# Loads of a backward recurrence: moved from SyncE's queue to ScalarE's, with an earlier compaction and a tile of its own for extra sums

## The chip, the cores and the metric

The kernel runs on one core of a Trainium2 chip. The metric is device time in microseconds (us) of one execution; lower is better. TensorE (PE) does matmuls and transposes, VectorE (DVE) and ScalarE (ACT) work element by element, GpSimd (POOL) does copies and issues DMAs, and SyncE (SP) only issues DMAs. "SPq", "ACTq" and so on in profile lines are the engines' sequencers.

## The reference

The inputs are x (2048 tokens of 640), a memory of 8 rows, the weights Wq, Wk, Wv, Wo (32 heads of 128) and the three weights of a gated feed-forward network. All are bfloat16. The forward function is

```
xn  = layernorm(x)
mem = mem0
for i in range(64):                      # segments of 32 tokens
    h = concat(mem, xn[32 i : 32 i + 32])          # 8 + 32 rows
    q, k, v = h Wq, h Wk, h Wv                     # 32 heads of 128
    p = softmax(mask(q k^T * 128**-0.5))           # memory rows see all, token rows are causal
    o = (p v) Wo
    mem, out[i] = o[:8], o[8:]
s = concat(out)
g = silu(FFN(xn))
y = x + s * g
```

The kernel returns y and the gradients of all nine inputs for a given gradient of y. The memory makes the forward pass a chain of 64 steps, and the backward pass a second chain of 64 steps in the other direction: the gradient of a segment's memory rows is needed before the segment ahead of it can be worked on.

## The kernel before

The kernel goes through stages, which the profile shows one after the other (times from the start of the span): layer norm and the network forward (0 to 370 us), the forward recurrence (370 to 1690), a prologue of the backward pass (to 1826), the backward sweep (`phase4_Abwd`, 1826 to 3240), the gradients of Wq, Wk, Wv and of the token rows (`phase6_Awgrads`, to 4330), that of Wo (to 4650), and the network's backward pass (to 4945).

**One step of the sweep**, `chain(t, gap)`, t from 63 down to 0, takes the gradient of the memory rows of its segment, already turned (`hx`, in profile rows the copy at L1335), and on TensorE does in this order:

- `packed_half` twice and `packed_sel`: the 8 rows times Wo, for all heads. VectorE and ScalarE copy the halves to `sg` (rows `gs` in the profile).
- `vgrad` (L1199): the value gradients of all 40 rows of the segment. Its first part multiplies the probabilities of the 32 token rows, `prx`, with their gradient rows `xr`; its second part multiplies those of the memory rows, `prm`, with `sg`. These value gradients "ride" in the step because the 8 memory rows of them go on along the chain.
- `dprob_m` (its bank at L1278): the gradient of the memory rows' probabilities, after VectorE has made `gmT` from `sg` (L1264). ScalarE copies the result to `dPT` (L1282).
- transposes of `dPT`, and VectorE's softmax gradient `gpr` ... `dS`; the key gradients `gkv`; a transpose of `dS` that ScalarE copies to `dST` (profile rows `dSTm`, L1306); the query gradients from `dST`.
- between these, the `packed_out` groups: value, key and query gradients times the turned weights, summed in one bank. `fold_add` (ScalarE copies one half, VectorE adds, L339 and L341) makes the sum `fs` (tile `fsum`), `fold_turn` (L357) turns it into the next step's input, and `fold_store` has POOL store it (to `GWO` and `GXV`, L348).

`load_g(t - 1)` fetches what the next step's vgrad needs: `xr` from `GOS` or `GX`, `prf` (the same tokens' probabilities, 256 KB, from `PR`) and four small `prm` loads from `PM`. `xr` and `prf` lie in one large tile, and the profile names both `gor`. `prx_copy(t - 1)` compacts `prf` to `prx` with two copies on POOL (L1192, L1193).

**The gaps.** The token rows' own work needs no chain, and is put into the steps' gaps by hand: 157 *units* (a tile of 120 rows and four heads each) pass through `ld` (loads on SP, ahead of time, into a ring of tiles), `turn` (transposes on TensorE, three ScalarE copies to `gvT` and `gOT`, a store by POOL to `VTD`), `dprob` (`gdp`, L1391), `dsoft` (VectorE, a store by POOL to `DSR`) and `gmem` (ScalarE copy `gks`, a store by POOL to `GXP`). `gap_of` says which unit does what in which gap:

```
G1: turn 2nd unit, gmem_ld last unit of t + 1, dprob 1st unit
G2: dprob 2nd, turn 3rd, dsoft 1st        G3: dsoft 2nd, gmem_ld 1st, extra every 4th step
G4: dprob 3rd, turn 1st of the next step  G5: gmem_ld 2nd     G6: dsoft 3rd
```

`extra(m, bank)` in every fourth step multiplies the value gradients of four steps' memory rows, collected in `lv`, with the turned Wv, adds the halves into a tile `fsum` and has POOL store it to `GXV`. The tag `fsum` has one buffer, which `gpr`, `gu`, the step's sum and the extra sum share.

**The order.** `in_order` fixes each engine's instructions in the sweep to the written order, so a statement's place in `chain` is its place in its engine's queue. DMAs are issued by the engine that they are written for: `nc.sync` is SP, `nc.scalar` is ScalarE, `nc.gpsimd` is POOL.

**The weight gradients.** `Fetch` loads 8 x 22 units, each with the softmax gradient `dS` (from `DSR`), the probabilities `Pr` and rows `g`, `q`, `k` into a ring of `NB` places of the tile `land`. TensorE transposes `dS` (L1648), multiplies the three kinds (`r6p`, L1658), ScalarE and VectorE copy the results, and later groups multiply them with the layer's input (L1715, L1736).

Of the kernel before, what the change touches and what calls it, by code (L numbers as in the profile page):

```python
# [9 lines left out]
BF16 = mybir.dt.bfloat16  # L10
# [313 lines left out]
def packed_out(k, pm, x, W, first, last, i0=0, i1=16):  # L324

    nq = x.shape[2]
    for i in range(i0, i1):
        for a in range(2):
            for b in range(2):
                h = 16 * a + i  # L330
                p0 = 32 * (2 * a + b)
                k.nc.tensor.matmul(pm[p0:p0 + nq, 0:320], x[:, h, :], W[:, h, 320 * b:320 * b + 320],  # L332
                                   start=(first and i == 0), stop=(last and i == 15),
                                   tile_position=(0, p0), skip_group_check=True)


def fold_add(k, pm, up, fs):

    k.nc.scalar.copy(up, pm[64:128, 0:320])  # L339
    for c in (0, 160):  # L340
        k.nc.vector.tensor_tensor(fs[:, c:c + 160], pm[0:64, c:c + 160], up[:, c:c + 160], ALU.add)  # L341
    return fs
# [746 lines left out]
def phase4_Abwd(k, out2, W0, W4, WT, own, ps, banks):  # L1089
    nc, tc = k.nc, k.tc  # L1090
    D, DC, S, H, HD, T = k.D, k.DC, k.S, k.H, k.HD, k.T
# [5 lines left out]
    for s in range(3):  # L1097
        t0 = (2, 0, 1)[s]
        n = (T - 1 - t0 + 2) // 3
# [10 lines left out]
    with tc.tile_pool(name="gst", bufs=1) as st, tc.tile_pool(name="gchain", bufs=1) as ch, \  # L1110
# [67 lines left out]
                nc.gpsimd.dma_start(rows[64 * a:64 * a + 8].rearrange("r (g c) -> r g c", g=2),  # L1178
                                    k.GOS[t // 4, 2 * a:2 * a + 2, 0:8, t % 4, :].rearrange("g r c -> r g c"))

        def load_g(t):
            tl, s = t // 3, t % 3
            nc.sync.dma_start(xr, k.g_rows(t))
            nc.sync.dma_start(prf, k.PR[tl][32 * s:32 * s + 32].rearrange("q (g h) c -> g q (h c)", g=4))
            for g in range(4):
                nc.sync.dma_start(prm[32 * g:32 * g + 8],
                                  k.PM[t, g // 2].rearrange("(q b h) c -> b q h c", q=8, b=2)[g % 2])

        def prx_copy(t):
# [11 lines left out]

        def extra(m, bank):
            packed_out(k, bank, lv, WvT, True, True)
            fs = fold_add(k, bank, up, ch.tile([64, 320], BF16, name="fsum", tag="fsum"))
            for b in range(2):
                nc.gpsimd.dma_start(k.GXV[128 * m:128 * m + 128, 320 * b:320 * b + 320].rearrange("(t r) d -> t r d", r=32)[:, 24:32],
                                    fs[32 * b:32 * b + 32, :])
# [26 lines left out]
        def chain(t, gap):  # L1234
# [30 lines left out]
                                      pg[:, :, 2 * a:2 * a + 2, :].rearrange("p j g q -> p q g j"))  # L1265
            vgrad(vb, sg, prm, 8, 4, 8, False)
            nc.sync.dma_start(k.GOS[t // 4, :, :, t % 4].rearrange("g r c -> (g r) c"), sg)
            if t > 0:
                load_g(t - 1)
            for g, e in ((0, 's'), (2, 'v'), (1, 's'), (3, 'v')):  # L1270
                k.copy(gv[:, 8 * g:8 * g + 8, :], vb[g], eng=e)
            nc.gpsimd.tensor_copy(lv[:, :, 8 * (t % 4):8 * (t % 4) + 8], gv[:, :, 32:40])
# [7 lines left out]
            dprob_m(1)  # L1280
            dPT = ch.tile([40, 2, P], BF16, name="dPT", tag="seq")
            nc.scalar.copy(dPT[:], psd.rearrange("p a q h -> p a (q h)"))  # L1282
            gap("G1")
            packed_out(k, pm, gv32, WvT, True, False, 0, 5)
            ps2 = bview(bC, P, 2, 40, bf=True)
# [36 lines left out]
            with nc.allow_non_contiguous_dma(reason="mem rows of dS"):  # L1322
                for a in range(2):
                    for (c0, c1, d0) in ((0, 8, nx + 8 * s), (8, 40, 32 * s)):
                        (nc.sync, nc.gpsimd)[a].dma_start(k.DSR[tl][nx + 8 * s:nx + 8 * s + 8, 16 * a:16 * a + 16, d0:d0 + c1 - c0],
                                                          dS[:, a, c0:c1])
            packed_out(k, pm, gkT, WkT, False, False, 4, 16)
            gap("G3")
            packed_out(k, pm, gqT, WqT, False, True)
# [5 lines left out]
                nc.vector.tensor_copy(goxs[(t - 1) % 2][:, :, 0:8], pt[:])  # L1335
            fold_store(nc.gpsimd, k.m_rows(k.GWO, t - 1) if t > 0 else out2f, fs)
            fold_store(nc.gpsimd, k.GXV[32 * t:32 * t + 24, :], fs, 8)
            if t > 0:
                prx_copy(t - 1)
            gap("G6")  # L1340

        uu = {}
# [102 lines left out]
        def gap_of(t):  # L1445
            def at(f, tt, i0, i1=None):
                b = batch.get(tt, ())
                for u in b[i0:i0 + 1 if i1 is None else i1]:
                    f(*u)

            def gap(g):
                if g == "W0":
                    ride_ld(t - 1)
                elif g == "G1":
                    at(turn, t, 1)
                    at(gmem_ld, t + 1, 2)
                    at(dprob, t, 0)
                elif g == "G2":
                    at(dprob, t, 1)
                    at(turn, t, 2)  # L1460
                    at(dsoft, t, 0)
                elif g == "G3":
                    if t > 0:
                        load_xp(t - 1)
                    at(dsoft, t, 1)
                    at(gmem_ld, t, 0)
                    if t % 4 == 0:
                        extra(t // 4, ps.tile([P, 512], F32, name="exb", tag="x", bufs=5))
                elif g == "G4":
                    at(dprob, t, 2)  # L1470
                    at(turn, t - 1, 0)
                elif g == "G5":
                    at(gmem_ld, t, 1)
                elif g == "G6":
                    at(dsoft, t, 2)
                if t == 0 and g == "G1":
                    fetch.append(Fetch(k, W0))
                if t == 0 and g in ("G1", "G2"):
                    fetch[0].to(2 if g == "G1" else 3)
                if t == 0 and g == "G3":  # L1480
                    fetch[0].w(0)
                for i in range(WARM.get(g, 0)):
                    nc.tensor.matmul((bA if g in ("W1", "G2") else bB)[:], k.ident[:], WqT[:, 0, 0:512], start=True, stop=True)
            return gap
# [41 lines left out]
        for i in range(len(pro) + 2):  # L1526
            for f, o in ((turn, 0), (dprob, 1), (dsoft, 1), (gmem, 2)):
                if 0 <= i - o < len(pro):
                    f(*pro[i - o])
                if f is not dsoft and not (f is dprob and i % 3):  # L1530
                    next(work, None)
            if 0 <= i - 2 and (i - 2 + 6 < len(pro) or i >= len(pro) - 2):
                ld_next()
            if 1 <= i < 17:
                h0 = 2 * (i - 1)
                nc.sync.dma_start(WvT[:, h0:h0 + 2, :], k.WVT[:, h0:h0 + 2, :])
            if i == 8:
                chain_consts()
                ride_ld(T - 1)
            if i == 16:  # L1540
                ride(T - 1)
            if i == len(pro):
                for _ in work:
                    pass
                loads(T - 1)
                load_q(T - 1)
                load_xp(T - 1)
                load_g(T - 1)
                prx_copy(T - 1)
        load_k(T - 1)  # L1550
        for t in range(T - 1, -1, -1):
# [8 lines left out]
class Fetch:  # L1560

    def __init__(self, k, W0):
        self.k, self.NB = k, 5
        NF = k.NTL - 2
        self.units = [(qd, tl) for qd in range(8) for tl in [NF, NF + 1] + list(range(NF - 1, -1, -1))]
        self.st, self.Ws, self.n = {}, {}, 0
        t = W0.tile([P, 5 * self.NB * 512 + 8 * k.D], BF16, name="land", tag="w0")
        four = lambda ap: ap.rearrange("p (h c) -> p h c", h=4)
        b = [[t[0:120, 512 * (5 * i + j):512 * (5 * i + j) + 512] for i in range(self.NB)] for j in range(5)]
        self.dS, self.P = [[four(x) for x in y] for y in b[0:2]]  # L1570
        self.rows = dict(zip("gqk", b[2:5]))
        c = 5 * self.NB * 512
        self.ws = [four(t[:, c + 4 * k.D * i:c + 4 * k.D * (i + 1)]) for i in range(2)]
# [10 lines left out]
    def ld(self, u):  # L1584
        k, nc = self.k, self.k.nc
        qd, tl = self.units[u]
        c0, h0 = qd * 512, qd * 4
        n = k.geo(tl)[3]
        dS, Pr = self.dS[u % self.NB], self.P[u % self.NB]
        nc.sync.dma_start(dS[0:n], k.DSR[tl][:, h0:h0 + 4, :])  # L1590
        nc.sync.dma_start(Pr[0:n], k.PR[tl][:, h0:h0 + 4, :])
        rw = []
        for nm in ("g", "q", "k"):
            r = self.rows[nm][u % self.NB]
            src = k.g_src(tl, c0, c0 + 512) if nm == "g" else k.x_src(tl, nm, c0, c0 + 512)
            k.load_x(r, 0, src, nc.sync)
            if nm == "q":
                t0, (ns, nm_, nx, n) = 3 * tl, k.geo(tl)
                nc.sync.dma_start(r[nx:n], k.QVM[t0:t0 + ns, :, qd // 2, 0, 512 * (qd % 2):512 * (qd % 2) + 512].rearrange("t r c -> (t r) c"))
            else:  # L1600
                k.load_m(r, tl, nm, c0, c0 + 512, nc.gpsimd)
            rw.append(r)
        self.st["l", u] = (dS, Pr, rw)
# [7 lines left out]
def phase6_Awgrads(k, X, W0, fetch, out0, out3, out4, out5):  # L1611
# [6 lines left out]
    NF = NTL - 2  # L1618
    NS = k.NR - 120 * NF
    R = 384  # L1620
    NB = 5
    assert NS == 8 * NF and NW == NF and (96 * NF) % R == 0 and S - 96 * NF == P
    st, Ws, cnt = fetch.st, fetch.Ws, dict(w=0, s=0, g=0, x=0)
    units, ld_to, ld_w = fetch.units, fetch.to, fetch.w
    with tc.tile_pool(name="h6i", bufs=3) as io, tc.tile_pool(name="h6", bufs=1) as hp, \
# [140 lines left out]
            s1(u0 + 2)  # L1766
            yield

        ld_to(5)
        for p in range(3):  # L1770
            gv_ld(p)
        for _ in head(0):
# [589 lines left out]
```

## Time and profile before

| | |
|---|---|
| median of 3 runs | 4944.16 us (4942.93 to 4951.85) |
| the profiled execution | 4946.79 us, of which the span 4944.8 us |
| mean granted TensorE clock | 0.945 |
| busy share of the span | PE 90%, PEld 57%, DVE 46%, ACT 32%, POOL 42% |
| instructions | 165433 |
| DMA | 853.19 MB, mean 173 GB/s |
| backward sweep, 1826 to 3240 us | PE busy 1169.17 of 1414 us, granted clock 0.86 |
| weight gradients, 3240 to 4330 us | PE busy 1015.63 of 1090 us, granted clock 0.98 |

The views of the profile are read like this. A row of waits says which engine stood still at which line, `<-` what released it, then the sum in us, how often, and the longest; "bank <- POOL prx" is a wait of a matmul into `bank` for POOL's writing of `prx`, and "DMA gor<-PR" is the landing of a transfer from `PR` into `gor`. A row of a timeline has start and duration in us, engine, line, operation, written from read tile, shape, and in square brackets the idle time before it with its releaser. The granted clock is the share of full speed that the throttle left to TensorE. Durations of DMA_DIRECT2D rows on an engine's queue are those of issuing, not of the transfer.

### The profile page before, as it was taken

The numbers are of one execution on the slowest core, as the hardware profiler recorded it, in microseconds if no ns is written. First come the engines' busy times: TensorE is split into PE (matmuls) and PEld (weight loads), VectorE is DVE, ScalarE is ACT, GpSimd is POOL, SyncE is SP. The second block draws the span as 40 slices with busy tenths as digits, with TensorE's granted clock in tenths as the row PEclk, the third lists the DMA queues.
The fourth block names the chain that finished last, engine by engine and source line by source line (L and its number), as shares of the span: only waits on it lengthen the run. The fifth ranks groups of instructions, "written<-read, shape, count | busy, mean of one in ns | idle before, by whom it ended". The sixth has DMA issues, their size and how long they took to land.

```text
span 4944.8 us, 165433 instructions
## 1 busy us (share of the span) xinstructions
PE 4464.1 (90%) x66872; PEld 2806.8 (57%) x66872; DVE 2257.3 (46%) x7188; ACT 1576.9 (32%) x4328; POOL 2075.0 (42%) x3512
## 2 busy tenths in 40 slices
PE   8998999999998878887778888879999999999999
PEld 4545555555555545555555555555555666667675
DVE  8635666666665344443434444343333333411461
ACT  5433555555444323222222222222222222200000
POOL 6533555555555134444434444353333333311440
PEclk9999999999999988888888888889999999999999
DMA  8774666666555776666655655585444555559783
GB/s 273 220 248 123 177 179 181 179 180 182 168 169 167 166 208 178 186 182 176 176 165 168 170 167 168 146 201 139 132 133 130 145 151 151 179 169 230 161 188 95
DMA packets 1004226, 853.19 MB, mean 173 GB/s; under 512 B 527910, under 2 KB 870490, under 8 KB 1001500
## 3 DMA queue, kind: packets, MB, share of 16 engines
q1 hardware_dynamic: 798227, 572.69, 42.0%
q0 software_dynamic: 122960, 221.40, 15.0%
q10 hardware_dynamic: 82275, 48.52, 3.8%
q8 instruction: 528, 8.65, 0.8%
q14 instruction: 236, 1.93, 0.1%
HBM read 496.51 MB, written 304.56 MB: 162 GB/s over the span
## 4 chain that ended last, share of the span: by engine, by line
PE 40%; DMA 12%; issue 5%; POOL 4%; DVE 3%; SPq 1%; ACT 1%; ACTq 0%; POOLq 0%; DVEq 0%
PE wg L1736 10%; PE bank L332 6%; PE g L1715 4%; DMA land<-DSR 4%; PE oa L1884 4%; PE wa L2272 2%; PE bank L313 2%; PE r6p L1658 1%; PE pgxb L2205 1%; DMA GXV<-fsum 1%; PE bank L1278 1%; PE t6g L1691 1%; DMA kT<-QVS 1%; DMA kT<-GOS 1%; PE t L1648 1%
## 5 line engine op out<-in xcount | busy, mean ns | idle before, releaser
L1736 PE MATMUL wg<-gr,hr 128*128 128x512 bf16 x2400 | 521.7, 379 | 0.3 <-DMA hr<-HRO 0.3
L313 PEld LDWEIGHTS <-hx 128*32 128x32 bf16 x10240 | 256.0, 99 | 251.6 <-issue 49.6
L1736 PEld LDWEIGHTS <-hr 128*128 128x128 bf16 x2400 | 233.9, 98 | 279.3 <-DMA hr<-HRO 0.6
L1715 PE MATMUL g<-land,ghacc 128*128 128x320 bf16 x2048 | 326.7, 305 | 0.0
L1378 POOL DMA_DIRECT2D VTD<-gvT x176 | 126.5, 719 | 420.4 <-ACT gvT L1377 396.3
L90 DVE CAST wgo<-wg 128x512 bf16<-128x512 f32 x72 | 49.8, 692 | 471.7 <-PE wg L1736 471.7
L90 DVE CAST stg<-bank 128x512 bf16<-128x512 f32 x256 | 177.1, 692 | 157.4 <-PE bank L313 154.2
L886 POOL DMA_DIRECT2D OR<-xv x163 | 89.8, 551 | 364.2 <-ACT xv L92 341.6
L332 PE MATMUL bank<-WvT,gv 128*32 128x320 bf16 x4096 | 233.6, 390 | 0.0
L1715 PEld LDWEIGHTS <-ghacc 128*128 128x128 bf16 x2048 | 193.1, 99 | 65.8
L1673 POOL DMA_DIRECT2D GSP<-grs x48 | 25.5, 542 | 466.0 <-ACT grs L1665 466.0
L818 ACT ACTIVATE xP<-xsp,xnm 120x120 bf16<-120x120 f32 (+1 forms) x540 | 186.6, 374 | 26.4 <-DVE xnm L800 23.6
L313 PE MATMUL bank<-WoT,hx 128*32 128x512 bf16 x2560 | 183.0, 441 | 11.8 <-DVE hx L1335 11.1
L838 POOL TENSOR_TENSOR xP<-xP,xrz 120x480 bf16<-120x480 bf16 x163 | 161.1, 989 | 64.9 <-DVE xrz L837 40.3
L92 ACT CAST wgo<-wg 128x512 bf16<-128x512 f32 x48 | 28.1, 586 | 465.4 <-PE wg L1736 394.4
L246 POOL DMA_DIRECT2D land<-KS x256 | 144.9, 571 | 65.9 <-PE r6p L1658 51.0
L332 PE MATMUL bank<-Wo,oTm 128*32 128x320 bf16 x4032 | 154.5, 307 | 18.9 <-DVE oTm L689 18.8
L92 ACT COPY ghacc<-t6g 128x384 bf16<-128x384 bf16 (+1 forms) x176 | 82.6, 469 | 275.5 <-PE t6g L1691 272.7
L332 PE MATMUL bank<-WkT,kT 128*8 128x320 bf16 x4096 | 161.5, 299 | 2.8 <-DVE kT L1245 1.7
L313 PE MATMUL bank<-Wq,hx 128*32 128x512 bf16 x2560 | 161.6, 381 | 0.0
L313 PE MATMUL bank<-Wv,hx 128*32 128x512 bf16 x2560 | 161.6, 381 | 0.0
L332 PEld LDWEIGHTS <-gv 128*32 128x32 bf16 x4096 | 120.8, 120 | 63.7
(392 smaller groups left out, 10832.0 us busy)
## 6 DMA issues: line engine op xcount, KB each, us to landing
QVS<-stg SPq DMA_DIRECT2D x128, 256.0 KB
kT<-VTD SPq DMA_DIRECT2D x64, 320.0 KB
PR<-xP POOLq DMA_DIRECT2D x168, 120.0 KB
VTD<-gvT POOLq DMA_DIRECT2D x168, 120.0 KB
land<-DSR SPq DMA_DIRECT2D x168, 120.0 KB
land<-PR SPq DMA_DIRECT2D x168, 120.0 KB
OR<-xv POOLq DMA_DIRECT2D x163, 120.0 KB
orr<-OR SPq DMA_DIRECT2D x14, 1280.0 KB
```

Of the source, the lines that this page charges most:

```text
L90: return nc.vector.tensor_copy(out, in_)
L92: return nc.scalar.copy(out, in_)
L246: eng.dma_start(d, src if src.shape[0] > 1 else src[0])
L313: k.nc.tensor.matmul(bank[32 * g:32 * g + 32, :], x[:, dc, :], W[:, dc, c0:c0 + 512], start=(dc == 0), stop=(dc == k.DC - 1), tile_positio ...
L332: k.nc.tensor.matmul(pm[p0:p0 + nq, 0:320], x[:, h, :], W[:, h, 320 * b:320 * b + 320], start=(first and i == 0), stop=(last and i == 15), ...
L818: nc.scalar.activation(Pb[0:n, j, 0:n], sp[0:n, j, :], ACT.Exp, bias=nmx[0:n, j:j + 1], scale=k.scale, accum_out=Z[0:n, j:j + 1])
L838: eng.tensor_tensor(Pb[0:n, :, 0:n], Pb[0:n, :, 0:n], bc_last(rz[0:n], n), ALU.mult)
L1378: nc.gpsimd.dma_start(k.VTD[tl][:, :, h0:h0 + 4, :], vTq[:])
L1715: nc.tensor.matmul(pg[:], ring[:, i, j, r0:r0 + P], Ws[qd][i][:, j, 320 * h:320 * h + 320], start=(i == 0 and j == 0), stop=(i == 1 and j ...
L1736: nc.tensor.matmul(pw[:], hr[:, tl, dc * P:(dc + 1) * P], grs[i][:, tl, :], start=(tl == 0), stop=(tl == NF - 1))
L1884: nc.tensor.matmul(ac[j][i][:], orr[:, w, jj * P:(jj + 1) * P], gow[:, w, 320 * i:320 * i + 320], start=(w == 0), stop=(w == NW - 1))
L2272: nc.tensor.matmul(accs[i][:], xn_all[:, tt, dc * P:(dc + 1) * P], gtok[:, tt, 432 * f:432 * f + 432], start=(tt == 0), stop=(tt == NT - 1))
```

## The change

- `load_g(t - 1)` gets the queue as an argument. In the steps ScalarE issues it, right behind its copy to `dPT`; before, SP issued it behind the store to `GOS`. `prf` is now loaded ahead of `xr`. The first load, ahead of the sweep, stays on SP.
- `prx_copy(t - 1)` moves from the end of the step to its middle, behind the stores of the memory rows of `dS` and ahead of the second part of the key gradients' `packed_out`.
- `extra` writes its sums to the first 64 partitions of `lv`, no longer to a tile of tag `fsum`.
- `dprob` of a step's first unit moves from gap G1 to gap W1, behind vgrad and ahead of `dprob_m`.
- `Fetch` has six places for five, so one more unit is loaded ahead. Of a unit's loads, `Pr` and the `g` rows are issued by ScalarE; SP keeps four.

```diff
-        def load_g(t):
+        def load_g(t, q):
             tl, s = t // 3, t % 3
-            nc.sync.dma_start(xr, k.g_rows(t))
-            nc.sync.dma_start(prf, k.PR[tl][32 * s:32 * s + 32].rearrange("q (g h) c -> g q (h c)", g=4))
+            q.dma_start(prf, k.PR[tl][32 * s:32 * s + 32].rearrange("q (g h) c -> g q (h c)", g=4))
+            q.dma_start(xr, k.g_rows(t))
             for g in range(4):
-                nc.sync.dma_start(prm[32 * g:32 * g + 8],
+                q.dma_start(prm[32 * g:32 * g + 8],
                                   k.PM[t, g // 2].rearrange("(q b h) c -> b q h c", q=8, b=2)[g % 2])
...
         def extra(m, bank):
             packed_out(k, bank, lv, WvT, True, True)
-            fs = fold_add(k, bank, up, ch.tile([64, 320], BF16, name="fsum", tag="fsum"))
+            fs = fold_add(k, bank, up, lv[0:64].rearrange("p h c -> p (h c)")[:, 0:320])
...
             nc.sync.dma_start(k.GOS[t // 4, :, :, t % 4].rearrange("g r c -> (g r) c"), sg)
-            if t > 0:
-                load_g(t - 1)
...
             nc.scalar.copy(dPT[:], psd.rearrange("p a q h -> p a (q h)"))
+            if t > 0:
+                load_g(t - 1, nc.scalar)
             gap("G1")
...
                         (nc.sync, nc.gpsimd)[a].dma_start(k.DSR[tl][nx + 8 * s:nx + 8 * s + 8, 16 * a:16 * a + 16, d0:d0 + c1 - c0],
                                                           dS[:, a, c0:c1])
+            if t > 0:
+                prx_copy(t - 1)
             packed_out(k, pm, gkT, WkT, False, False, 4, 16)
...
             fold_store(nc.gpsimd, k.GXV[32 * t:32 * t + 24, :], fs, 8)
-            if t > 0:
-                prx_copy(t - 1)
             gap("G6")
...
+                elif g == "W1":
+                    at(dprob, t, 0)
                 elif g == "G1":
                     at(turn, t, 1)
                     at(gmem_ld, t + 1, 2)
-                    at(dprob, t, 0)
...
-                load_g(T - 1)
+                load_g(T - 1, nc.sync)
...
-        self.k, self.NB = k, 5
+        self.k, self.NB = k, 6
...
-        nc.sync.dma_start(Pr[0:n], k.PR[tl][:, h0:h0 + 4, :])
+        nc.scalar.dma_start(Pr[0:n], k.PR[tl][:, h0:h0 + 4, :])
...
-            k.load_x(r, 0, src, nc.sync)
+            k.load_x(r, 0, src, nc.scalar if nm == "g" else nc.sync)
...
-    NB = 5
+    NB = fetch.NB
...
-        ld_to(5)
+        ld_to(NB)
```

## The prediction

> **What bounds the kernel now.** I read the table by stage first, then TensorE's waits, then the queues behind the longest of them. In the table by stage the columns after the window are its length and the busy time (count) of PE, PEld, DVE, ACT and POOL, then the granted clock, the DMA share and GB/s. The backward sweep and the weight gradients are the two stages that the diff touches:
>
> ```profile
> 1826.00:3240.00 1414.00, 1169.17 (x28160) 778.34 (x28160) 574.84 (x2863) 391.63 (x1150) 599.47 (x1143) 0.86 0.60 169
> 3240.00:4330.00 1090.00, 1015.63 (x8742) 648.91 (x8738) 407.00 (x893) 293.26 (x577) 422.34 (x753) 0.98 0.55 152
> ```
>
> TensorE sets both ends: 83% busy in the sweep, 93% after it. What a change can bring at an equal clock is its idle time, 245 us and 74 us. The sweep is 64 steps of 22.0 us. TensorE's waits name the idle time (total, times, longest):
>
> ```profile
> PE bank L1199 <- POOL prx L1193: 98.9, 40, 11.8
> PE t L1648 <- DMA land<-DSR: 55.9, 51, 4.2
> PE bank L357 <- DVE fsum L341: 44.0, 36, 4.3
> PE gvpt L1374 <- DMA kT<-QVS: 29.7, 16, 3.3
> PE bank L1278 <- DVE gmT L1264: 20.2, 55, 0.5
> PE gvpt L1374 <- DMA kT<-QVX: 12.0, 9, 2.6
> ```
>
> The first is the compaction of the probabilities. The timeline of POOL, then of PE, at the seam of two steps:
>
> ```profile
> 2103.97 1.04 POOL L348 DMA_DIRECT2D GWO<-fsum  x2
> 2104.99 1.02 POOL L348 DMA_DIRECT2D GXV<-fsum  x2
> 2106.01 0.41 POOL L1192 COPY prx<-gor 128x256 bf16<-128x256 bf16 x1
> 2106.35 0.24 POOL L1193 COPY prx<-gor 128x64 bf16<-128x64 bf16 x1
> ```
>
> ```profile
> 2106.64 0.17 PE L1199 MATMUL bank<-prx,gor 32*128 32x40 bf16 x1 [1.60 <-POOL prx L1193]
> ```
>
> The copies stand behind four store issues of 2.06 us that need the step's last sum; their input landed long before. TensorE idles 1.60 us for them. The unit loads (kT rows) are late because of SP's queue, which the waits of SP in the sweep show:
>
> ```profile
> SPq L1365 <- DMA gor<-PR: 100.4, 38, 3.9
> SPq L1174 <- DMA gor<-PR: 62.4, 25, 4.6
> SPq L272 <- DMA gor<-GOS: 58.5, 25, 3.1
> SPq L1174 <- DMA gor<-GOS: 37.3, 16, 3.5
> ```
>
> Lines L1365, L272 and L1174 load other tiles, yet wait for the landing of load_g's (the gor rows). In the built program all DMAs of SP and ScalarE take eight completion semaphores in turn, and an issue waits until the last DMA of its semaphore has landed. With the two gor<-GX rows (21.3 and 10.2) this is 290 us, 4.5 us per step.
>
> **The change part by part.**
>
> *Compaction in mid step.* It removes 98.9 us of waits. The copies (0.65 us) now wait for the landing of prf. On SP's ring it came 9.35 us (median) after the issue, worked out from issue and semaphore times; issued at the end of the dPT copy, that is some 12 us ahead of the next seam. POOL's stores queued behind them (DSR, GXP, VTD, then GWO and GXV) are late by up to 4 us, and the last two still follow the last sum. Next late at the seam is ScalarE's copy of sg (vgrad's second half); in steps without the wait, vgrad's first matmul came 0.04 us after that copy began. I take −95; bounds −107 (8 us of waits named otherwise at the same line) and −80.
>
> *Place for the extra sums.* One step in four writes two sums in one tile, and the second waits for the store of the first: 53.9 us of VectorE's waits in the sweep, 13 times. TensorE's L357 wait in these steps is 34.9 of the 44.0 (summed by step). Gone: −35, bounds −38 and −28. lv is next written about 10 us later, when its stores have landed.
>
> *dprob into W1.* Its eight matmuls stand where TensorE waited for gmT: 20.2 us in 55 steps. Part of the steps carry no first unit: −14, bounds −20 and +5 (dPT comes later by dprob where the wait was short).
>
> *load_g off SP.* SP loses, per step, 0.59 + 0.57 + 4 × 0.36 = 2.6 us of issue and waits of 4.5 us. Late unit loads cost TensorE 29.7 + 12.0 and, for GOS rows and the line's rest, 8: 49.7. I take −34; bounds −49.7 and −10, as ScalarE's DMAs take the same semaphores and SP may now wait on them at other lines.
>
> *load_g on ScalarE.* This is the cost. After dPT the queue of ScalarE is
>
> ```profile
> 2089.09 0.37 ACT L1282 CAST dPT<-bank 40x256 bf16<-40x256 f32 x1 [0.56 <-PE bank L1278]
> 2089.61 0.24 ACT L1376 COPY gvT<-gvpt 128x96 bf16<-128x96 bf16 x1
> 2089.74 0.48 ACT L1377 COPY gvT<-gvpt 128x384 bf16<-128x384 bf16 x1
> 2090.11 0.58 ACT L1383 COPY xqT<-ggpt 128x480 bf16<-128x480 bf16 x1
> 2094.31 0.27 ACT L1306 COPY dSTm<-bank 104x128 bf16<-104x128 bf16 x1 [3.62 <-PE bank L1304]
> ```
>
> The six issues come between the first row and the second. At the issue times of ScalarE elsewhere (0.36 to 0.41 each) they take some 2.4 us, which the idle 3.62 us ahead of dST covers: turn copies 1.3 and one of 0.25 then end near dPT + 4.0, and dST starts at dPT + 5.1. Behind them wait dprob of the second unit (TensorE, needs gvT and xqT), the query gradients (need dST) and POOL's VTD store. But the fourth to sixth issue reuse semaphores. Going through the built program's waits step by step, about 18 steps have a PM load wait for the landing of the same step's own prf and xr; some 5 for own prf behind a transpose; some 20 for the GOS store and a unit load; the rest for next to nothing. xr landed 7.4 us and prf 9.35 us after the issue behind SP's other loads. ScalarE's own ring holds less, so I take them landed at dPT + 7 to 9. The turn copies, the 0.25 us copy and dST then end at dPT + 9 to 10.5 instead of 5.4: 3.6 to 5.2 us lost on the path, 4.4 in the middle. 18 × 4.4 = 79; 5 × 1.5 = 7; 20 × 0.6 = 12 (GOS stores landed 3.5 us after their issue); 21 × 0.6 = 13 for the issues alone: +111. Bounds: 0 (all landed within dPT + 3, the idle time) and 64 × 4.4 = +280 (every step waits for its own loads).
>
> *Weight gradients.* 55.9 of the 74 us idle wait for dS of a unit, the first load in SP's row of six. Two of six issues (0.40 of some 2.6 us each) go to ScalarE, and there is one more unit of reach. A unit takes some 3.3 us of SP and of TensorE's fast parts, and ScalarE has 1.2 + 0.7 us idle beside 1.65 us of copies, against 0.8 of issues. I take −20; bounds −60 and +40, the latter if 176 units' copies of r6p are late by 0.23 us each.
>
> **Two rules beside the rows.** The loads' landing decides the cost above. The Trainium skill, DMA: Bandwidth & Descriptors, section "Issuing engines are not separate DMA queues", says that DMAs of all issuers run on the same 16 engines, and that another issuer saves only the sequencer's issue time. By it the landings stay 7.4 and 9.35 us, and the load_g term would be nearer 18 × 5 = 90 than 79; it speaks against the change, and SP's 290 us of waits would only move.
>
> The granted clock is 0.86 in the sweep, with 0.98 to 1.00 in most others. A step with 0.63 us of idle PE was granted 0.70 (window, PE busy, ..., clock):
>
> ```profile
> 1908.80:1930.50 21.70, 21.07 (x444) 13.34 (x443) 9.94 (x52) 6.75 (x20) 9.41 (x19) 0.70 0.54 162
> ```
>
> while a step with 2.02 us of idle in 15.30 (3201.7 to 3217.0) had 1.00. So I count no gain from a higher clock. TensorE: Matmul & The Clock Gate, Part 1, makes idle windows of about 3.4 us the cause of a halved clock; by that rule the removed waits would also raise the clock, and ScalarE's holds of 4 us lower it; to bring 0.86 to 0.98 would be worth 1169 × (1 − 0.86 / 0.98) = 143 us, which this trace's steps don't support.
>
> **Sum.** −95 − 35 − 14 − 34 + 111 − 20 = −87. From the profiled execution (span 4944.8, with 2.0 around it 4946.79) this gives 4860; that execution lies 2.6 us above the median of 4944.16, so 4857 against the median.
>
> **The rivals.** *ScalarE's issues hold nothing* (the loads land early on a ring of their own, or the waited-for semaphores are free): +111 falls to some +15, giving 4857 − 96 = 4761. For it: 3.62 us idle ahead of dST, and the small load of that ring. Against: the program's waits, and 9.35 us of landing.
>
> *ScalarE's hold decides* (slower): the PM loads wait in most steps for prf and xr, and dST, gvT and with them TensorE's G2 gap come late. The gains sum to 198 us, 3.1 us per step; the hold must average more than that. At 3.8 us, 64 × 3.8 = 243: 4944 + 45 = 4989. For it: SP's waits on exactly these DMAs, 4.5 us per step, were harmless on a queue without copies, and would now stand in front of copies. Against: ScalarE issues few DMAs, so its semaphores are mostly SP's, which land in about 3 us.
>
> *The wait is replaced* at the seam by the sum's store or by late unit loads: prx at half (+48), unit loads at nothing (+34), weight gradients at 0 (+20): 4857 + 102 = 4959; with one of these less, no change. For it: POOL is later by the landing.
>
> **How the numbers follow.** Forecast 4857, its own range 4805 to 4925: 0.44. Nothing held, 4720 to 4805: 0.20. Around no change, 4925 to 4960: 0.10. Hold decides, above 4960: 0.26. A difference of 0.2% (10 us) is about what a measurement of this kernel can tell. Faster than 4934: 0.44 + 0.20 + 0.02 = 0.66; same 0.04; slower 0.04 + 0.26 = 0.30. The range leaves out 0.1 at each end: 4765 to 4995.
>
> **What would show it.** Right: the prx wait gone from TensorE's list, L357 near 10 us, SP's gor rows gone; on ScalarE, gvT waits for DMA landings in some 20 steps, with dST 4 us late there; the sweep near 1347 us, the weight gradients near 1070. Wrong: holds in most steps or in none; new waits of TensorE for xqT, dSTm or POOL; a weight gradient stage that gets longer; a sweep clock that moves by over 0.03.

## The result, and the profile after

The changed kernel takes 5072.32 us (median of 4 runs, 5059.44 to 5074.77), the kernel before 4943.55 beside it: a ratio of 1.0254, 95% interval 1.0231 to 1.0277. It is 2.5% slower, by some 127 us; 4857 was forecast. Its profiled execution has a span of 5073.1 us.

The two stages again, in the table by stage (window, length, busy time and count of PE, PEld, DVE, ACT and POOL, granted clock, DMA share, GB/s); the bounds have moved with the stages:

```profile
1826.00:3340.00 1514.00, 1160.29 (x28148) 758.57 (x28152) 576.70 (x2863) 384.94 (x1149) 595.57 (x1142) 0.86 0.57 158
3340.00:4461.00 1121.00, 1026.35 (x8777) 657.23 (x8766) 404.73 (x894) 291.44 (x578) 423.83 (x754) 0.97 0.54 149
```

The sweep has 100 us more, the weight gradients 31 us more (rounded bounds). Measured between fixed instructions, the sweep from its first to its last turned input `hx` grew from 1388.7 to 1478.5 us with TensorE's idle time in it from 237.8 to 339.9, and the weight gradients from the first transpose of dS to the last from 1043.2 to 1070.7. TensorE's waits over the span:

```profile
PE gdp L1391 <- ACT xqT L1383: 282.2, 59, 10.9
PE r6p L1659 <- ACT gr L1666: 47.8, 46, 3.7
...
PE bank L357 <- DVE fsum L341: 11.7, 27, 0.9
PE bank L1199 <- DMA gor<-GX: 11.6, 1, 11.6
```

The waits of before are gone but for one: no row for prx, L357 at 11.7 for 44.0, and in the sweep gmT at 1.8 for 20.2 and kT<-QVS at 2.3 for 29.7. The 11.6 us at L1199 stand at the first vgrad of the sweep, and stood there before too, as 11.8 of the 98.9 us for prx. In place of the others stands one row larger than all the waits of before together: the dprob of a step's second unit waits for ScalarE's turn copy, 4.8 us each, 59 times. ScalarE's timeline in one step says why:

```profile
2033.53 0.36 ACT L1280 CAST dPT<-bank 40x256 bf16<-40x256 f32 x1 [0.56 <-PE bank L1276]
2033.59 0.53 ACTq L1183 DMA_DIRECT2D gor<-PR  x1
2034.16 0.53 ACTq L1184 DMA_DIRECT2D gor<-GX  x1
2034.78 8.96 ACTq L1186 DMA_DIRECT2D prm<-PM  x4
2043.84 0.24 ACT L1376 COPY gvT<-gvpt 128x96 bf16<-128x96 bf16 x1 [9.94 <-DMA kT<-PM]
2043.97 0.48 ACT L1377 COPY gvT<-gvpt 128x384 bf16<-128x384 bf16 x1
2044.34 0.58 ACT L1383 COPY xqT<-ggpt 128x480 bf16<-128x480 bf16 x1
```

and TensorE's of the same step:

```profile
2044.97 0.20 PE L1391 MATMUL gdp<-gvT,xqT 128*128 128x24 bf16 x1 [7.34 <-ACT xqT L1383]
```

The four PM issues last 8.96 us, not 1.7 (the median of the steps in which no semaphore was held): by the times of the single issues the third came 5.64 us after the copy to dPT, when this step's own prf had landed at 5.62, and the fourth at 9.58, when its own xr had landed at 9.50. They waited for the completion semaphores that these two transfers still held. The idle time in the bracket names a transfer that happened to land last; the engine had in fact been in its queue. TensorE was ready for xqT 3.7 us after the copy to dPT.

### The profile page after: what moved, and what is told of

It is laid out like the page before. It is cut to its first block, busy times and chain, and to the rows that moved or that the text cites. A ratio compares the mean times of both kernels' runs of the same rounds, so it can differ in the third digit from the quotient of the medians.

```text
span 5073.1 us, 165199 instructions
## 1 busy us (share of the span) xinstructions
PE 4463.8 (88%) x66872; PEld 2794.2 (55%) x66872; DVE 2257.7 (45%) x7188; ACT 1566.7 (31%) x4328; POOL 2072.4 (41%) x3512
## 4 chain that ended last, share of the span: by engine, by line
PE 39%; DMA 18%; issue 3%; DVE 2%; ACT 2%; SPq 1%; POOL 1%; ACTq 1%; POOLq 0%; DVEq 0%
PE wg L1737 10%; PE bank L332 8%; PE oa L1885 3%; PE g L1716 3%; PE bank L313 2%; PE wa L2273 2%; DMA prm<-PM 2%; PE pgxb L2206 2%; DMA land<-PR 1%; DMA land<-DSR 1%; DMA land<-QVM 1%; PE r6p L1659 1%; DMA gor<-PR 1%; DMA kT<-QVM 1%; DMA xP<-PR 1%
## 5 line engine op out<-in xcount | busy, mean ns | idle before, releaser
L1391 PE MATMUL gdp<-gvT,xqT 128*128 128x24 bf16 (+1 forms) x704 | 73.8, 186 | 282.3 <-ACT xqT L1383 282.2
L332 PE MATMUL bank<-WkT,kT 128*8 128x320 bf16 x4096 | 238.1, 396 | 1.6 <-DVE kT L1245 1.6
L1391 PEld LDWEIGHTS <-xqT 128*128 128x128 bf16 x704 | 53.1, 98 | 305.2 <-ACT xqT L1383 291.0
L1659 PE MATMUL r6p<-land 120*128 120x128 bf16 (+1 forms) x1408 | 112.3, 225 | 90.5 <-ACT gr L1666 47.8
L1376 ACT COPY gvT<-gvpt 128x96 bf16<-128x96 bf16 (+1 forms) x176 | 41.4, 235 | 483.9 <-DMA prm<-PM 224.2
L332 PE MATMUL bank<-WvT,gv 128*32 128x320 bf16 x4096 | 185.0, 326 | 3.8 <-issue 3.5
L1666 ACT CAST gr<-r6p 120x512 bf16<-120x512 f32 x160 | 93.7, 585 | 271.9 <-DMA land<-PR 64.2
```

The lines of the kernel that those rows point to most:

```text
L1391: nc.tensor.matmul(dp[:, j, nx:n], gOT[:, j, :], vTq[:, :, j, 0:8], start=True, stop=True)
L1659: nc.tensor.matmul(pr[:, j * P:(j + 1) * P], lh[0:n, j, :], rw[i][0:n, j * P:(j + 1) * P], start=True, stop=True)
```

## The experiments

All ratios are against the kernel before, which took 4954 to 4957 us beside them; the sweep and weight-gradient times are measured in the profiled executions as above (before: 1388.7 with 237.8 idle, and 1043.2).

| kernel | us | ratio (95%) | sweep, idle in it | weight gradients |
|---|---|---|---|---|
| a_sp | 4942.59 | 0.9975 (0.9963 to 0.9987) | 1344.1, 219.1 | 1080.2 |
| b_act | 5207.70 | 1.0507 (1.0490 to 1.0525) | 1619.7, 424.3 | 1044.1 |
| b_fetch | 4985.19 | 1.0060 (1.0041 to 1.0080) | 1402.0, 247.4 | 1078.0 |
| a_pmsp | 4960.41 | 1.0009 (0.9992 to 1.0025) | 1375.7, 231.2 | 1081.5 |
| a_pmfirst | 4983.25 | 1.0044 (1.0025 to 1.0062) | 1374.1, 224.6 | 1071.0 |
| a_pool_f5 | 4850.56 | 0.9774 (0.9754 to 0.9795) | 1288.8, 173.5 | 1049.6 |
| b_pxexdp | 4948.12 | 0.9977 (0.9964 to 0.9989) | 1382.4, 229.5 | 1047.7 |
| b_pxexdpnb | 4936.47 | 0.9946 (0.9929 to 0.9963) | 1374.4, 218.4 | 1042.0 |
| b_exdp | 4950.05 | 0.9987 (0.9974 to 1.0001) | 1379.8, 214.1 | 1051.9 |
| a_pmpool | 4906.30 | 0.9898 (0.9874 to 0.9923) | 1305.2, 183.1 | 1088.4 |
| a_pool_nb6 | 4841.39 | 0.9758 (0.9725 to 0.9790) | 1293.4, 180.5 | 1043.3 |
| a_pool_nb6_g4 | 4824.92 | 0.9737 (0.9701 to 0.9773) | 1269.3, 162.2 | 1044.7 |

Names that begin with a_ start from the changed kernel, those with b_ from the one before. My theory was that ScalarE's queue is held by load_g's issues. The rivals were the compaction in mid step (it holds POOL), the transfers themselves, and the Fetch.

**load_g on ScalarE, alone (b_act)**

```diff
             nc.sync.dma_start(k.GOS[t // 4, :, :, t % 4].rearrange("g r c -> (g r) c"), sg)
-            if t > 0:
-                load_g(t - 1)
...
             nc.scalar.copy(dPT[:], psd.rearrange("p a q h -> p a (q h)"))
+            if t > 0:
+                load_g(t - 1, nc.scalar)
```

> The kernel before with one part alone: load_g on ScalarE behind dPT, prf ahead of xr. Theory: the hold comes with this part alone. TensorE reaches the second unit's dprob some 1 us later than in the changed kernel (the first unit's dprob is still in G1), so about 3.6 us per step are lost at L1391 instead of 4.5: +200 to +240, less the SP relief of 30 to 50: 5080 to 5150 us. Rival (the hold needs the compaction in mid step or the six-place Fetch): 4880 to 4960 us.

It is 251 us slower (5207.70 against 4956.86), more than the forecast of this run. The row is there with nothing else of the change:

```profile
PE gdp L1391 <- ACT xqT L1383: 274.0, 46, 10.7
PE bank L1199 <- POOL prx L1193: 58.1, 41, 3.1
```

The hold needs neither compaction, nor Fetch, nor the earlier dprob. The other parts of the change made it cheaper, not dearer: 5072 with them, 5208 without. In this program 38 of 63 steps have a PM issue wait for the step's own prf and another for its own xr, where the changed kernel has 18, and these 38 make up 260 of the 273 us lost behind dPT. TensorE was also busy 44 us longer in the sweep with the same work (1195 for 1151), at a granted clock of 0.81 for 0.86.

**The Fetch, alone (b_fetch)**

```diff
-        self.k, self.NB = k, 5
+        self.k, self.NB = k, 6
...
-        nc.sync.dma_start(Pr[0:n], ...)
+        nc.scalar.dma_start(Pr[0:n], ...)
...
-            k.load_x(r, 0, src, nc.sync)
+            k.load_x(r, 0, src, nc.scalar if nm == "g" else nc.sync)
...
# and NB = fetch.NB for 5 where the units are used
```

> The kernel before with the Fetch part alone (six places, Pr and g rows issued by ScalarE). Theory: the weight gradients' stage is longer by some 27 us for itself, from TensorE's waits at r6p for ScalarE's copies, where it waited for dS before: 4955 to 4985 us. Rival (that stage was longer only because of what the sweep left behind, or its gain is hidden by it): 4910 to 4945 us.

28 us slower. The stage is 35 us longer in the profiled execution, the slowest of the four, and 27.5 in the changed kernel. TensorE's first wait in the stage is no longer for dS, but for ScalarE's copy; behind that stands a wait of ScalarE's own. TensorE's list in the stage, then ScalarE's:

```profile
PE r6p L1658 <- ACT gr L1665: 54.5, 34, 5.4
```

```profile
ACT gr L1665 <- DMA land<-PR: 73.7, 39, 4.1
```

**The PM loads elsewhere (a_pmsp, a_pmpool), or first (a_pmfirst)**

```diff
# a_pmsp                                # a_pmpool: the same with nc.gpsimd
-                q.dma_start(prm[32 * g:32 * g + 8],
+                nc.sync.dma_start(prm[32 * g:32 * g + 8],
...
# a_pmfirst: the loop over g ahead of
             q.dma_start(prf, ...)
             q.dma_start(xr, ...)
```

> The changed kernel with the four PM loads back on SP; prf and xr stay on ScalarE behind dPT. Theory (the third to sixth issue wait for semaphores of transfers still under way, the first two hardly): ScalarE is held 1.1 to 2 us per step instead of 7.3, TensorE's L1391 row falls from 282 to under 60 us: 4800 to 4870 us. Rival (the issues of the two large loads, or their landing, are what holds): L1391 stays over 150 us and the time over 4950 us.

> The changed kernel with load_g's six issues in another order on ScalarE: the four PM loads first, then prf, then xr. Same transfers, same queue, same count. Theory (ScalarE is held because the last PM issues reuse completion semaphores of the large loads just issued, and of SP's transfers): now the last two issues reuse those of the small PM loads or of earlier SP transfers, the hold falls from 7.3 to 4 to 5 us a step and TensorE's L1391 row from 282 to 80 to 150 us: 4900 to 4980 us. Rival (what holds is the count of issues, or the load on the transfer engines): within 25 us of the changed kernel, L1391 over 230 us.

> The changed kernel with the four PM loads on POOL; prf and xr stay on ScalarE, Fetch as changed. Theory (the PM issues were held by semaphores that SP and ScalarE share; on SP they held SP, and the unit loads came late; POOL's DMAs take others): L1391 under 25 us and L1374 under 60 us, 4850 to 4900 us with Fetch's 28 us in it. Rival (two large loads on ScalarE are enough to make SP's or ScalarE's queue late): 4930 us or more.

With the PM loads off ScalarE, its last issue ended 1.6 us after dPT (median, for 7.55 in the changed kernel) and L1391 fell from 282 to 10 us: half of the expectation for a_pmsp was right. The time was not; 4960 us is no gain over before. The late work is now SP's, and TensorE waits for unit loads (its waits in the sweep):

```profile
PE gvpt L1374 <- DMA kT<-QVS: 64.1, 25, 6.9
PE gvpt L1374 <- DMA kT<-QVX: 40.9, 15, 7.3
PE ggpt L1381 <- DMA kT<-GOS: 28.7, 18, 3.0
```

With the same four small loads on POOL (a_pmpool) these three rows fall to 44.0, 16.1 and 13.4, L1391 stays at 8.0, and the sweep is 70 us shorter than in a_pmsp. The total, 4906, lies 6 us above the end of what I expected. So the choice of queue for four loads of 5 KB is worth 1.1% between SP and POOL (ratios 1.0009 and 0.9898), and 3.6% between ScalarE and POOL (1.0254 and 0.9898, each against the runs of before beside it).

In a_pmfirst the same six issues on the same queue, in another order, take 2.1% off (1.0044 for 1.0254; L1391 118.9 for 282.2). That excludes the number of issues and the transfer load as the main cause. 4983 lies 3 us above the expectation: unit loads and GOS stores of SP that land late still hold the issues, the third and fourth most of all.

**load_g back on SP (a_sp), and the other sweep parts without it (b_pxexdp, b_exdp)**

```diff
# a_sp
             nc.sync.dma_start(k.GOS[t // 4, :, :, t % 4].rearrange("g r c -> (g r) c"), sg)
+            if t > 0:
+                load_g(t - 1, nc.sync)
...
-                load_g(t - 1, nc.scalar)
# b_pxexdp: the kernel before, with the hunks of prx_copy, extra and W1 alone
# b_exdp:   the kernel before, with those of extra and W1 alone
```

> The changed kernel with load_g back on SP, behind the store to GOS (prf ahead of xr as in the change); all other parts as changed. Theory (ScalarE's queue held by the load_g issues, 281 us of TensorE's waits at L1391 for xqT): that row falls under 15 us, the sweep loses some 230 us against the changed kernel, the weight gradients keep their +27 us: 4800 to 4880 us. Rival (the compaction in mid step holds POOL, or the transfers themselves have become slower): over 5000 us, with TensorE's idle time in the sweep about as in the changed kernel.

> The kernel before with three parts alone: compaction in mid step, place for the extra sums, dprob in W1; load_g on SP with xr first, Fetch as before. Theory (SP's queue is the next bound behind the removed waits, so that their 144 us come back as late unit loads, and Fetch costs some 28 us on its own): TensorE's L1374 row rises from 42 to 110 to 140 us and the time is that of the run with load_g on SP less 28: 4900 to 4930 us. Rival (the gains are eaten by something that belongs to prf ahead of xr or to Fetch): under 4880 us.

> The kernel before with the place for the extra sums and dprob in W1 alone; the compaction stays at the end of the step, load_g on SP, Fetch as before. Theory (with load_g on SP it is the compaction in mid step that gives its gain back: POOL stands 161 us waiting for prf there and its late GXP stores hold ScalarE): these two parts alone bring most of their 35 + 14 us, 4895 to 4920 us, faster than the three parts together. Rival (any gain in the sweep comes back at SP's queue, whatever the part): 4935 to 4955 us, with the L1374 row over 75 us.

These are the misses that taught most. a_sp had no row at L1391 over 2 us, yet came out at 4943, not 4800 to 4880: its sweep is 45 us shorter than before, its weight gradients are 37 us longer. Three parts that remove 163 us of named waits bring 8 us together (b_pxexdp, 0.23%), and two of them nothing that this run can tell (b_exdp, interval up to 1.0001). The first rows of TensorE in a_sp and then b_pxexdp:

```profile
PE gvpt L1374 <- DMA kT<-QVS: 86.4, 27, 5.0
...
PE gvpt L1374 <- DMA kT<-QVX: 48.9, 14, 5.3
```

```profile
PE bank L321 <- ACT gs L92: 80.4, 31, 4.8
...
PE gvpt L1374 <- DMA kT<-QVS: 53.2, 28, 5.5
PE gvpt L1374 <- DMA kT<-QVX: 25.6, 18, 3.8
```

In a_sp the unit loads are late (135 us for 42). In b_pxexdp, where prf is issued last of the two large loads, POOL also stands 161.0 us in mid step for its landing ("POOL prx L1192 <- DMA gor<-PR", 46 times; 56.1 us, 20 times in a_sp); its late GXP stores make ScalarE's gks wait 238.7 us, and the copy of sg behind that is the new row at L321. In the sweep these two programs differ only in the order of prf and xr, and the one with prf first is 38 us shorter there (1344.1 for 1382.4, one profiled execution each). The rise at L1374 that I expected for b_pxexdp, 110 to 140 us, was 79. But the compaction isn't all that eats the gains: without it (b_exdp) 25 us come back at the seam, prx at 124.3 us in 55 places for 98.9 in 40. And of the 24 us of idle time that did go (214.1 for 237.8), 15 were lost again, as TensorE was busy longer with the same work (1166 for 1151) at a granted clock of 0.84 for 0.86. My theory for b_exdp has fallen. Its rival was right on the time; the row that it named (L1374 over 75 us) was 49.3, and the wait showed at L1199. In all three SP's waits for load_g's landings stay at 260 to 282 us (before: 277, same window).

**load_g on POOL (a_pool_f5), with the sixth place (a_pool_nb6), with the compaction later (a_pool_nb6_g4)**

```diff
-                load_g(t - 1, nc.scalar)
+                load_g(t - 1, nc.gpsimd)
# and the Fetch: a_pool_f5 as before; a_pool_nb6 six places, all hardware issues on SP
# a_pool_nb6_g4:
-            if t > 0:
-                prx_copy(t - 1)
             packed_out(k, pm, gkT, WkT, False, False, 4, 16)
...
             fs = fold_add(k, pm, up, ch.tile([64, 320], BF16, name="fsum", tag="fsum"))
+            if t > 0:
+                prx_copy(t - 1)
             gap("G4")
```

> The changed kernel with load_g issued by POOL at the same place, and with the Fetch of before (five places, all on SP). Theory: neither ScalarE nor SP carries these issues, so the gains of the compaction, the extra sums and the earlier dprob are there and the unit loads are not late: TensorE's rows L1391, L1199 and L1374 each under 25 us, 4760 to 4860 us. Rival (POOL, with 3.3 us more of issues per step and a compaction that waits for the landing, becomes the bound): new waits for VTD, GXP or prx of over 80 us, 4880 us or more.

> The changed kernel with load_g on POOL, and six places in the Fetch with all its issues on SP. Expected from the parts: the run with load_g on POOL less 6 to 12 us of the sixth place: 4835 to 4850 us. If the sixth place brings nothing there: 4850 to 4860 us.

> The same with the compaction between the step's last sum and gap G4, ahead of the sum's stores, for mid step. Theory (in mid step POOL stands some 85 us for prf's landing with DSR and VTD stores behind, and late GXP stores hold ScalarE's gks for 300 us): POOL's waits for gor landings fall under 30 us, TensorE's L357 row from 50 to 25 us, 4805 to 4840 us. Rival (the copies, 0.65 us, now stand ahead of the sum's stores, and those are what is late next): no faster than with the compaction in mid step.

On POOL the loads hold neither queue: L1391 is 1.3 us, L1199 has no row for prx, L1374 none for landings, and the sweep has 64 us less idle time than before and is 100 us shorter; the other 36 us are TensorE's busy time with the same work, at a granted clock of 0.92 for 0.86. 4851 us, 2.3% faster than before. L357 is no shorter than before (50.4 for 44.0); why is open. POOL does wait for its own semaphores ("POOL DSR L1409 <- DMA gor<-PR", 49.9 us), but apart from the sweep's first vgrad no wait of TensorE there of over 1 us ends with POOL or with a landing. With the sixth place it is 4841; the two intervals overlap. The later compaction gives the lowest median, 4824.92 us, 2.6% faster than before, but this interval and that of a_pool_nb6 overlap as well, so that the later place is better than mid step isn't shown. Its mechanism isn't either: TensorE's L357 row went from 55.3 to 47.3, not to 25, and POOL's waits for gor landings stayed over 100 us.

**The sixth place on SP (b_pxexdpnb)**: b_pxexdp and

```diff
-        self.k, self.NB = k, 5
+        self.k, self.NB = k, 6
...
# and NB = fetch.NB for 5 where the units are used
```

> The same three parts and six places in the Fetch, with all its issues on SP. Theory (ScalarE's issues in the weight gradients are what delays its copies of r6p; the sixth place is free or helps): the weight gradients within 10 us of before or up to 25 us shorter, 4880 to 4925 us. Rival (the sixth place or its larger tile costs by itself): 15 us or more slower than the kernel with the three parts alone, waits for ScalarE's copies at r6p as in the changed kernel.

12 us faster than b_pxexdp, the stage 6 us shorter, and the row "r6p <- ACT gr" is not among its waits; the total is 11 us over what I expected. The larger ring costs nothing, so what is left of the Fetch to cost its 28 us is ScalarE's two issues per unit. No run has these alone.

## Why the prediction was wrong, point by point

**The removed waits: right in the change, for another reason than I gave.** In the changed kernel prx went from 98.9 to the 11.6 at the sweep's first vgrad, L357 in the sweep from 43.2 to 10.8, gmT from 20.2 to 1.8, unit and GOS loads from 48.9 to some 5: 182 us, where the sum had 178. The −95 counted that first wait as one at a seam. The sum took each row as worth its own length. The runs with load_g on SP show that this holds only while something else slows the step or SP is relieved: there 163 us of rows brought 8, or 45 in the sweep with prf first. Two readings were off without weight: a step took 22.4 us (1388.7 / 62), not 22.0, and a landing 9.35 us behind dPT is 10 us ahead of the next vgrad (median), not 12.

**The load_g term: the step that failed.** I had +111, measured are 281 us at L1391. Step by step, from the end of the copy to dPT to ScalarE's next copy, and TensorE's wait:

| steps | forecast loss each | measured hold | measured loss each | sum |
|---|---|---|---|---|
| 18 that wait for their own prf and xr | 4.4 | 10.5 | 8.0 | 144 for 79 |
| 31 others, held by a landing | 0.6 to 1.5 | 7.4 | 4.2 | 130 for some 25 |
| 13 with free semaphores | 0.6 | 2.7 | 0.55 | 7 for some 8 |

The 18 steps are those that the program's waits had named; the 31 others make up the larger part of the miss, 105 of 170 us. Three things were mis-sized. The need: I measured the delay at dST (dPT + 5.1), but TensorE needs xqT for the second unit's dprob first, at dPT + 3.7, and the earlier dprob of the first unit had brought that forward by about 1 us (in b_act, without it, the steps that wait for prf and xr lose 6.8 us at a hold of 10.3). The landings: xr came at dPT + 9.7 (median), behind prf on the same ring at 5.9; I had 7 to 9 for both. And the middle class was priced as if SP's transfers were issued and landed as before. In 27 of these steps it was SP's transfers that held the issue, for 132 us in all, 43 of them for GOS stores; the stores that held it for over 1 us landed 5 to 9 us after their issue, not 3.5. SP's queue itself waited 414 us for landings in the sweep (307 before), among them those of ScalarE's loads:

```profile
SPq L1365 <- DMA gor<-PR: 55.7, 19, 6.5
SPq L1168 <- DMA gor<-GOS: 42.0, 14, 4.0
```

So in the changed kernel the two queues held each other in turn. A loss of this size doesn't need that: in b_act SP's transfers held ScalarE's issues for 3.5 us in all.

**The rivals.** "ScalarE's hold decides" is what happened, with 4.5 us per step (281 over 62) where 3.1 was the turning point; I gave it 0.26 and 4989 us. The argument that I set against it, that ScalarE's semaphores are mostly SP's and land in about 3 us, is the mistake above. "Nothing held" is what the loads on POOL give (4851), though not as low as 4761.

**The weight gradients: wrong sign**, +27.5 for −20. The row for dS went as expected; the copies of r6p became late instead, which the upper bound (+40) had. ScalarE's 0.8 us of issues fitted its idle time on average, but an issue that waits up to 4 us for a landing doesn't: in b_fetch 178 of the 345 issues waited, 156 us in all, most for ScalarE's own `Pr` loads (49) and SP's from `QVM` (38).

**The clock.** That I counted no gain fits this change by the mean, 0.86 before and after; the reason that I gave doesn't hold. Across the runs the clock moved, here in b_act, before and in a_pool_nb6_g4:

```profile
1860.00:3130.00 1270.00, 932.36 (x21269) 608.87 (x21270) 447.21 (x2237) 300.64 (x894) 468.83 (x892) 0.81 0.53 147
1860.00:3130.00 1270.00, 1051.75 (x25160) 701.46 (x25152) 527.29 (x2656) 359.71 (x1058) 551.72 (x1048) 0.86 0.61 174
1860.00:3130.00 1270.00, 1107.51 (x27661) 730.13 (x27664) 567.70 (x2845) 383.57 (x1136) 815.99 (x1503) 0.93 0.73 186
```

TensorE's busy time in the sweep for the same work goes from 1195 (b_act) over 1151 (before) to 1107 us (a_pool_nb6_g4). And the step of 0.70 with 0.63 us of idle time was misread, as the clock answers late. Cut where the clock changes, the start of that stretch of the kernel before reads

```profile
1904.70:1908.10 3.40, 0.70 (x12) 0.45 (x8) 0.55 (x2) 1.33 (x4) 1.01 (x2) 1.00 0.71 142
1908.10:1921.70 13.60, 13.06 (x231) 8.09 (x235) 5.32 (x24) 3.20 (x9) 5.35 (x11) 0.50 0.51 163
```

The idle time that this half clock follows, 2.69 us at L357, lies in the step before, and from 1921.7 us on the clock is full again. From 1860 to 3130 us the clock of this kernel is full or half, in windows of 3.41 us. Of the full windows in which TensorE was busy for less than half, 36 of 37 are followed by a half one; of those with 90% and more, none of 148 (in the changed kernel 40 of 40 and 5 of 167). So removed waits can bring clock too. The mean follows from how the idle time is bunched, and not from its sum alone: in the same window the changed kernel has 270 us of it in 56 stretches of over 1 us, the kernel before 163 in 72, and both have 0.86.

The Trainium skill, TensorE: Matmul & The Clock Gate, Part 1, has an idle window of about 3.4 us halve the clock. The length agrees with this trace; here a window that was still busy for up to half was enough.

**The rule on issuers.** The Trainium skill, DMA: Bandwidth & Descriptors, "Issuing engines are not separate DMA queues", has another issuer save only issue time. I left it out of the sum; by my own figure for it (90 for 79) the sum would have been −76, still the wrong sign. What the runs show of the landings agrees with it: they went by the order of the two large loads more than by the queue. The first landed 7.4 us after its issue before (xr on SP), 6.7 in a_sp (prf on SP) and 6.2 in the changed kernel (prf on ScalarE), the second 9.4, 8.8 and 9.3 us. My guess that ScalarE's emptier ring would land them sooner was worth little.

## What to carry to other kernels

A DMA issue in a compute engine's queue is an in-order instruction that can wait for a completion semaphore: before it is moved there, list per step whose landing each issue waits for, and price the copies behind it by the time at which their first reader stands ready. Removed waits add up only as far as the next queue allows; try the removal with that queue untouched, and move the load that fills it to the queue behind which nothing is needed soon (here POOL's, 2.3% faster, where ScalarE's was 2.5% slower). Small transfers deserve the same care as large ones: four loads of 5 KB, by place and order alone, moved this kernel by 2 to 4%.

## What the runs showed of the hardware that I had not expected

Issuing on ScalarE was cheap in itself: 0.52 to 0.53 us for a large load and 0.31 for a PM load (medians), 2.7 us from dPT to the next copy for all six with free semaphores; on POOL the same issues took 0.72 and 0.52 us, 3.5 us when back to back, and the sweep was 190 us shorter (1288.8 for 1478.5). The price of an issue lay in what it waited for and in what stood behind it.
